# Attention and mixture of experts: another instruction order, V on two hardware rings, smaller weight pieces and later Q/K loads

## The chip, the cores and the metric

The kernel runs on one core of one Trainium2 chip. The metric is the device time of one execution, in microseconds (us); lower is better. A "fast" or "slow" run below is one run as against the fastest of the same kernel: a run over 1.5% above that is called slow, and ratios use fast runs only.

A core has a matrix engine (PE), a vector engine (DVE), an activation engine (ACT), a general engine (POOL) and a synchronization engine (SP). Sixteen DMA engines move data. In this kernel POOL, SP and ACT can start DMAs; each of the three has a queue of its own in the profile (q0 for POOL, made by software; q1 for SP and q10 for ACT, in hardware).

## The reference

Eight batches, eight heads, sequence 576, head size 64. Attention has a decay per position (a cumulative sum of logarithms of f); its output goes through one of eight experts, chosen per batch.

```python
log_f = np.log(np.clip(f, 0.0001, 1.0))
cum = np.cumsum(log_f, axis=-1)
scores = q @ k^T / 8 + cum[:, :, :, None] - cum[:, :, None, :]   # causal
attn = softmax(scores)
x = attn @ v                              # (8, 576, 512) over all heads
# mixture of experts, one expert per batch:
e_idx = np.argmax(x.mean(axis=1) @ w_gate, axis=1)
out[b] = gate[b] * (np.maximum(x[b] @ w1[e_idx[b]], 0) @ w2[e_idx[b]])
```

(Shortened; the exponentials of the decay are applied to V and to the row sums in the kernel.)

## The kernel before

The program writes its own instruction order. Each piece of work is an `Op` with an engine, a duration, what it waits for and a priority; `Order.run` simulates the engines and the transfers, takes at each moment the ready piece with the lowest priority number, and emits its instructions. A group is four heads of one batch, so there are 16 groups. The steps of a group are: load Q and K (POOL's queue), transpose them (DVE), scores (PE), exponentials (ACT), mask (POOL), V times the decay (POOL, "weighing"), PV (PE), normalization (ACT, DVE). After two groups comes the batch's gate (PE), then the load of the chosen expert's W1 and W2 (POOL's queue), then 128 matmuls of W1 and of W2 ("MoE").

```python
    def load_v(b, c):                       # five chunks per batch, all from SP
        t = VF[od.slot(("vf", b))]          # two buffers
        if c < 4:
            nc.sync.dma_start(t[:, c, :, :], v[b, :, P * c:P * c + P, :].rearrange("h p e -> p h e"))
        ...
    # [cut] Q/K loads: four buffers, on POOL's queue
    raws[g, j] = od.add(f"raw{g}{j}", "POOL", .6, ..., takes=(("raw", g),) ..., lands=1.55, ...)
    # [cut] W1 and W2 of a batch: 4 KB and 8 KB pieces, on POOL's queue too
    nc.gpsimd.dma_start(W1[w].rearrange("p (q t) n -> p q (t n)", t=2), src.rearrange("p q t n -> p q (t n)"))
    nc.gpsimd.dma_start(W2[w].rearrange("p m n -> p (m n)"), ...)
    # [cut]
    pm = 1000 + 20 * b                      # priority of the MoE: after everything else
    for g in range(5, NQ):
        raws[g, 1].behind = [ld2]           # Q/K of later groups only wait for batch 0's weights
```

## Time and profile before

| | before |
|---|---|
| median of three runs | 280.07 us (276.8 to 280.75); with a fourth, of 281.22 us, it is 280.41 |
| profiled run: span | 281.3 us |
| PE busy | 242.6 us, 86% |
| wait of POOL for V | 18.4 us |
| first gate, last gate, end | 36.0, about 225.7, 281.3 us |

The lines below are from the page of the kernel before: the span; the busy time of each engine; the busy tenths of PE, the granted clock of PE and the share of the DMA engines in 40 slices of the span; the two data queues (packets, megabytes, share of the time of 16 engines); the chain that ended last, by engine.

```profile
span 281.3 us, 7976 instructions
...
PE 242.6 (86%) x3351; PEld 156.6 (56%) x3351; DVE 110.7 (39%) x298; ACT 175.1 (62%) x263; POOL 115.2 (41%) x181
...
PE   8976898892299599939889999989999999999990
...
PEclk9995799997589999986979999999999999999997
DMA  6946929999999999989999954931593259603122
...
q0 software_dynamic: 8880, 26.22, 49.1%
q1 hardware_dynamic: 43744, 19.04, 27.8%
...
PE 62%; DMA 17%; ACT 7%; POOL 4%; issue 4%; DVE 2%; SPq 2%; POOLq 0%; ACTq 0%
```

PE is busy most of the time, but in the two slices from 63 to 77 us it is busy for only 2 tenths, and in the one from 120 to 127 us for 3; there the DMA row stands at 9. Another clue is the chain: 17% of the span is DMA.

The next lines are waits of the kernel before: engine, line and tile, then what it waited for, then us in total, how many times, and the longest.

```profile
POOL vb L374 <- DMA vf<-in_v_dram: 18.4, 4, 11.6
PE ps_w L390 <- POOL e L361: 15.2, 3, 7.6
...
PE ps_s L348 <- ACT e L354: 7.1, 8, 1.4
```

POOL waited four times for V, up to 11.6 us at once. The chain of work that ended last, in order of time (start, us, what), has the same loads in it:

```profile
43.77 26.98 DMA vf<-in_v_dram
...
104.17 19.87 DMA vf<-in_v_dram
```

By stretches of the span (start:end, length, busy time of PE, PEld, DVE, ACT and POOL with the number of instructions, granted clock, DMA share, GB/s):

```profile
44.00:71.00 27.00, 18.40 (x344) 12.89 (x337) 11.70 (x35) 16.90 (x23) 14.23 (x23) 0.92 1.13 203
71.00:80.00 9.00, 4.45 (x58) 2.65 (x58) 2.40 (x6) 2.41 (x4) 8.69 (x13) 0.50 1.03 192
98.00:160.00 62.00, 53.83 (x916) 35.59 (x919) 31.60 (x88) 44.35 (x60) 37.05 (x57) 0.92 1.07 227
160.00:226.00 66.00, 64.99 (x1004) 43.00 (x993) 33.05 (x92) 43.67 (x59) 21.70 (x34) 1.00 0.55 127
226.00:282.00 56.00, 48.54 (x342) 35.46 (x341) 2.25 (x8) 30.60 (x62) 1.27 (x2) 0.96 0.41 112
```

A DMA share over 1 means that packet times overlap. Up to 160 us the DMA engines are full and PE is not; from 71 to 80 us PE works for 4.45 of 9 us. After 160 us PE is full, and after 226 us only MoE is left: the last gate is followed by 55 us. The instances of the gate's matmuls (count; shortest, median and longest in ns; first and last start) give the ends of that count:

```profile
L470 PE MATMUL ps_w<-wg,pt x64: 172/256/277, 36.0 to 226.4; 128*128 128x8 f32 x64
```

From the timeline of PE, all eight gates start at 36.0, 62.8, 97.4, 119.7, 147.9, 169.6, 197.0 and 225.7 us. The start of the kernel is seen in two lines of PE's timeline (start, us, instruction):

```profile
12.53 0.52 PE L311 MATMUL ps_w<-identf,CUM 64*128 64x64 f32 x5
...
14.23 0.57 PE L348 MATMUL ps_s<-qt,kt 32*128 32x448 bf16 x8
```

The five transposes of the cumulative sum begin at 12.53 us, and the first scores at 14.23 us.

### The profile page before, as it was taken

The numbers are of one execution on the slowest core, as the hardware profiler recorded it, in microseconds if no ns is written. First come the engines' busy times: TensorE is split into PE (matmuls) and PEld (weight loads), VectorE is DVE, ScalarE is ACT, GpSimd is POOL, SyncE is SP. The second block draws the span as 40 slices with busy tenths as digits, with TensorE's granted clock in tenths as the row PEclk, the third lists the DMA queues.
The fourth block names the chain that finished last, engine by engine and source line by source line (L and its number), as shares of the span: only waits on it lengthen the run. The fifth ranks groups of instructions, "written<-read, shape, count | busy, mean of one in ns | idle before, by whom it ended". The sixth has DMA issues, their size and how long they took to land.

```text
span 281.3 us, 7976 instructions
## 1 busy us (share of the span) xinstructions
PE 242.6 (86%) x3351; PEld 156.6 (56%) x3351; DVE 110.7 (39%) x298; ACT 175.1 (62%) x263; POOL 115.2 (41%) x181
## 2 busy tenths in 40 slices
PE   8976898892299599939889999989999999999990
PEld 3433654661154367624356756765686597695940
DVE  4663535472043665604266554556453310000000
ACT  2189375972166797834868754886487677493930
POOL 4057159930888586435656534362231210000000
PEclk9995799997589999986979999999999999999997
DMA  6946929999999999989999954931593259603122
GB/s 120 227 72 127 228 37 200 209 207 197 199 202 203 217 289 218 215 200 212 230 256 209 214 149 102 231 82 58 128 229 68 87 112 221 213 2 130 41 94 81
DMA packets 52666, 45.84 MB, mean 163 GB/s; under 512 B 39376, under 2 KB 41424, under 8 KB 51728
## 3 DMA queue, kind: packets, MB, share of 16 engines
q0 software_dynamic: 8880, 26.22, 49.1%
q1 hardware_dynamic: 43744, 19.04, 27.8%
q8 instruction: 28, 0.46, 0.7%
q14 instruction: 14, 0.11, 0.1%
HBM read 62.03 MB, written 9.44 MB: 254 GB/s over the span
## 4 chain that ended last, share of the span: by engine, by line
PE 62%; DMA 17%; ACT 7%; POOL 4%; issue 4%; DVE 2%; SPq 2%; POOLq 0%; ACTq 0%
PE ps_w L525 19%; PE ps_w L511 17%; DMA vf<-in_v_dram 17%; PE ps_w L390 10%; PE ps_s L348 6%; ACT e L354 5%; PE ps_w L587 4%; PE ps_w L528 3%; PE ps_w L470 2%; ACT e L357 2%; SPq L250 2%; POOL e L361 1%; POOL vb L374 1%; PE ps_w L270 1%; PE ps_s L270 1%
## 5 line engine op out<-in xcount | busy, mean ns | idle before, releaser
L354 ACT ACTIVATE e<-ps_s 128x1792 bf16<-128x1792 f32 (+2 forms) x60 | 90.7, 1512 | 26.1 <-PE ps_s L348 24.3
L511 PE MATMUL ps_w<-xT,w1e 128*128 128x288 bf16 x512 | 72.6, 291 | 2.6 <-DMA w1e<-in_moe_w_dram 1.4
L511 PEld LDWEIGHTS <-w1e 128*128 128x128 bf16 x512 | 60.7, 142 | 13.6 <-issue 9.0
L361 POOL TENSOR_SCALAR_AFFINE_SELECT e<-e 128x512 bf16<-128x512 bf16 x64 | 40.7, 636 | 58.2 <-ACT e L354 56.5
L525 PE MATMUL ps_w<-w2e,h1T 128*128 128x512 bf16 x256 | 61.3, 390 | 0.0
L517 DVE TENSOR_SCALAR h1T<-ps_w,gate_b 128x288 bf16<-128x288 f32 x58 | 29.1, 512 | 58.0 <-PE ps_w L511 57.8
L374 POOL TENSOR_TENSOR vb<-vf,WF 128x512 bf16<-128x512 f32 x29 | 30.0, 1042 | 29.5 <-DMA vf<-in_v_dram 18.4
L348 PE MATMUL ps_s<-qt,kt 32*128 32x448 bf16 (+3 forms) x720 | 33.9, 288 | 8.5 <-ACT e L354 7.1
L525 PEld LDWEIGHTS <-h1T 128*128 128x128 bf16 x256 | 24.1, 101 | 30.3 <-issue 5.9
L519 ACT ACTIVATE h1T<-ps_w,gate_b 128x288 bf16<-128x288 f32 x70 | 34.0, 500 | 5.6 <-PE ps_w L511 5.3
L406 DVE SCALAR_TENSOR_TENSOR xT<-ps_w,lr 128x256 bf16<-128x256 f32 (+1 forms) x64 | 26.7, 452 | 26.6 <-ACT lr L400 22.9
L537 ACT COPY otile<-ps_w 128x512 f32<-128x512 f32 (+1 forms) x30 | 16.5, 550 | 30.9 <-PE ps_w L525 28.8
L390 PE MATMUL ps_w<-e,WB 128*32 128x192 bf16 (+4 forms) x512 | 19.3, 272 | 16.2 <-POOL e L361 15.2
L348 PEld LDWEIGHTS <-kt 32*128 32x128 bf16 x768 | 16.5, 95 | 27.4 <-issue 24.6
L390 PE MATMUL ps_w<-e,vb 128*32 128x320 bf16 (+4 forms) x1024 | 30.9, 264 | 0.3 <-DVE h1T L517 0.3
L339 DVE STREAM_TRANSPOSE kt<-rawk 128x576 f32<-128x576 f32 x16 | 20.0, 1252 | 26.1 <-PE ps_s L348 21.9
L395 ACT ACTIVATE lr<-ps_w 128x256 f32<-128x256 f32 (+1 forms) x32 | 13.3, 414 | 19.6 <-PE ps_w L390 19.6
L390 PEld LDWEIGHTS <-WB 128*32 128x32 bf16 x512 | 11.1, 102 | 25.4 <-issue 22.1
L390 PEld LDWEIGHTS <-vb 128*32 128x32 bf16 x1024 | 22.4, 102 | 3.1 <-issue 0.6
L339 DVE STREAM_TRANSPOSE qt<-rawq 128x576 f32<-128x576 f32 x16 | 19.9, 1246 | 1.4 <-DMA rawq<-in_q_dram 1.4
L587 PE MATMUL ps_w<-still 128*128 128x512 bf16 x69 | 16.3, 380 | 0.0
L400 ACT ACTIVATE lr<-lr 128x256 f32<-128x256 f32 (+1 forms) x32 | 14.2, 444 | 1.0
(58 smaller groups left out, 138.3 us busy)
## 6 DMA issues: line engine op xcount, KB each, us to landing
vf<-in_v_dram SPq DMA_DIRECT2D x32, 256.0 KB, 7.0
w2e<-in_moe_w_dram POOLq DMA_DIRECT2D x8, 1024.0 KB, 13.9
out_dram<-otile SPq DMA_DIRECT2D x32, 256.0 KB, 2.7
w1e<-in_moe_w_dram POOLq DMA_DIRECT2D x7, 1024.0 KB, 9.1
rawk<-in_k_dram POOLq DMA_DIRECT2D x16, 288.0 KB, 9.1
rawq<-in_q_dram POOLq DMA_DIRECT2D x16, 288.0 KB, 9.5
vf<-in_v_dram SPq DMA_DIRECT2D x8, 128.0 KB, 12.7
w1e<-in_moe_w_dram POOLq DMA_DIRECT2D x4, 256.0 KB, 7.3
```

Of the source, the lines that this page charges most:

```text
L339: nc.vector.transpose(dst, raw)
L348: nc.tensor.matmul(ps[h][:, col:col + i1 - i0], kt[32 * h:32 * h + 32, KLO[c]:KLO[c] + P, r], qt[32 * h:32 * h + 32, i0:i1, r], start=(r = ...
L354: nc.scalar.activation(e, PS_S[:, :, 0:WIDTH[s]], AF.Exp, scale=0.125)
L361: nc.gpsimd.affine_select(out=e[:, :, 0:128], in_=e[:, :, 0:128], pattern=[[0, 4], [1, 128]], channel_multiplier=-1, base=0, compare_op=AL ...
L374: eng.tensor_tensor(vb[:, c, :, :], vf[:, c, h, :], WF[:, b, c, h].unsqueeze(3).to_broadcast([P, 2, 4, D]), op=ALU.mult)
L390: nc.tensor.matmul(ps[32 * h:32 * h + 32, lo - i0:hi - i0], lhs, e[s][:, h, col:col + hi - lo], start=(n == 0), stop=(n == len(parts) - 1) ...
L406: nc.vector.scalar_tensor_tensor(XT[od.slot(("x", b))][:, mm, i0:i1], ps[:, 0:i1 - i0], LN_SCALE, LR[od.slot(("lr", (g, blk)))][:, 0:i1 - ...
L511: nc.tensor.matmul(ps[:, 0:288], lhs, xT[:, m, 288 * half:288 * half + 288], start=(m == 0), stop=(m == 3))
L517: nc.vector.tensor_scalar(dst, ps[:, 0:288], g[:, 0:1], 0.0, op0=ALU.mult, op1=ALU.max)
L519: nc.scalar.activation(dst, ps[:, 0:288], AF.Relu, scale=g[:, 0:1])
L525: nc.tensor.matmul(ps, h[:, j, P * sb:P * sb + P], w2[:, j, :], start=(j == 0), stop=(j == 7))
L587: od.filler = lambda i: nc.tensor.matmul(PS_W[i], still[:, 0:P], still[:, 0:512])
```

## The change

Its intent was to keep V from waiting behind other transfers, and to spread the MoE over the kernel. Cut to its core:

```diff
+PM0 = 10.0
+LAG = 2
 ... class Order: the fluid model of DMA time (transfer) is replaced
-    def transfer(self, queue, at, us):
+    def advance(self, now):        # queues SP, ACT, POOL take turns by descriptor;
+        ...                        # each queue has its own descriptor time ("grain")
+        busy["PE"] = 2.0           # and fillers cost .43 at first, .24 later
-    def load_v(b, c):
+    def load_v(op, b, c):
+        eng = nc.scalar if op.engine == "ACT" else nc.sync
-            loads_v[b, c] = od.add(f"v{b}{c}", "SP", 0.5, ...)
+            loads_v[b, c] = od.add(f"v{b}{c}", "ACT" if c % 2 else "SP", .4 if c % 2 else .5, ..., grain=.022)
-        for i in range(12):        # twelve fillers ahead of everything
-            nc.tensor.matmul(PS_S[:, i, :] if i < 4 else PS_W[i % 4], still[:, 0:P], still)
 ... W1 and W2 of batches 1 to 7: two DMAs each, packets of 2 KB
+            for q in range(2):
+                nc.gpsimd.dma_start(W1[w].rearrange("p (t q) n -> p q t n", t=2)[:, q], src[:, q])
+            for a in range(2):
+                nc.gpsimd.dma_start(W2[w].rearrange("p (b a c) n -> p a b (c n)", b=2, a=2)[:, a], src[:, a])
-        pm = 1000 + 20 * b
+        pm = PM0 + 6 * b           # units of W1: pm + .4 * j; of W2: pm + 3.4 + .5 * n
-                raws[g, 1].behind = [ld2]
+                raws[g, 1].behind = [ld2] if g < 6 else [wvs[g - LAG][0]]   # Q/K wait for V's weighing two groups earlier
 ... some durations of the model are re-measured
```

## The prediction

> **What bounds the kernel now.** The page: span 281.3 us, PE busy 242.6, of which 21 are filler matmuls. Real PE work is about 197 us, an estimate from durations in the chain of waits (0.49 us per four 288-column matmuls, 1.68 per 72 PV matmuls, 8.0 per output batch). The DMA queues took 49.1% + 27.8% + 1%, some 219 us. Neither alone explains 280. The table by stretches shows DMA share 1.03 to 1.13 from 44 to 160 us, with PE busy only 4.5 of 9 us at 71 to 80 (clock 0.50). The chain names V's load: 27.0 us at 43.8, 19.9 us at 104.2. From 160 us PE is 98% busy, and the span ends with 55 us of MoE alone, left over by its low priority.
>
> **Why V is slow.** The packet records show strict turns: at 66 to 75 us, some 80 packets per us of 2304 B (Q/K, 0.195 us each) alternate with 80 to 90 of V's 256 B (0.022 us); beside 4 KB weight packets V gets some 48. A batch of V is 288 packets per DMA engine: 6.3 us alone, 62 us against a Q/K stream (288 x 0.217). This agrees with the Trainium skill, "DMA: Bandwidth & Descriptors", section "Queues, rings and completion order": each DMA engine goes round robin between the queue rows that have work, by packet.
>
> **What the change does.**
> 1. Two V packets per software turn instead of one, and weight packets of 2 KB (about 0.17 us, half of the 4 KB packet's 0.353) instead of 4 and 8 KB (0.627). Estimate of V's rate: six times beside W2, 1.8 times beside Q/K.
> 2. Q/K loads wait for V's weighing two groups earlier, so no longer run ahead of V.
> 3. MoE is interleaved. After the last gate 20 + 48 + 64 + 48 MoE matmuls remain, about 26 us, against 55.
> 4. 20 fillers precede the first score matmul instead of 43; CUM was ready at 7.9 us, its transposes ran at 12.5 behind fillers. Saves 3 to 4 us.
> 5. Cost: 16 V issues on ACT. On SP the first two issues of a batch took 0.38 and 0.58 us, the next 2.9 and 10.8. With two per batch I expect about 0.5 each, 8 us of an engine 62% busy: off the path. Bytes are unchanged; W2's smaller packets add about 3 us of DMA work, POOL gets 14 more issues of about 0.6 us.
>
> **Sum.** Gate 0 at 33 us instead of 36. Per batch PE needs 24.6 us and DMA about 27 us of packet time (25 with overlap); I expect 26 per gate, so the last gate near 216 instead of 226, then 31 us plus waits for the last weights. **Predicted 250 us, 238 to 265.** Faster by over 2%: 0.93, within: 0.05, slower: 0.02.
>
> **What would show it.** (1) POOL's wait for V falls from 18.4 us to under 6; the chain holds little V; two 256 B packets per software packet. (2) DMA share less saturated before 160 us, higher after. (3) Last gate to end about 31 us. (4) First score matmul near 11 us. (5) V issues on ACT under 1 us. A new wait: MoE's first matmuls on w1e, 1 to 3 us in some batches, since they follow their gate by some 12 us of PE work, and w1e now takes 9.1 us to land.
>
> **What would make it wrong.** ACT issues that block for many us and hold up the exponentials; interleaved MoE stalling PE, which runs in order, on weights that land late, because every software byte shares one queue; DMA as the true bound (219 us plus start and tail), which would hold the time above 260.

Two readings of it need a note. The clock of the packet records begins 10.4 us before the span, so its "66 to 75 us" is 56 to 65 us of the span. And its "80 packets per us" are over all 16 engines.

## The result, and the profile after

The kernel after takes 264.94 us (median of four runs, 262.53 to 266.27). The ratio to the kernel before is 0.9469, with a 95% interval of 0.9364 to 0.9573. (Ratios here are the mean time of one kernel's fast runs over that of the other's of the same rounds, so they are not quite the ratios of the quoted medians.) The sign was right; the size was about half of the 30 us predicted: 264.94 lies at the top end of the range of 238 to 265.

The same lines of the page of the kernel after:

```profile
span 263.9 us, 7930 instructions
...
PE 235.2 (89%) x3325; PEld 152.6 (58%) x3325; DVE 110.9 (42%) x297; ACT 174.9 (66%) x261; POOL 128.2 (49%) x195
...
PE   7778998939999999499899976799999999999991
...
PEclk9975999988999999799999997999999999999998
DMA  6988979991999999954999998695997299049832
...
q0 software_dynamic: 13584, 26.22, 55.6%
q1 hardware_dynamic: 27104, 14.85, 22.5%
q10 hardware_dynamic: 16640, 4.20, 8.1%
...
PE 53%; DMA 21%; ACT 8%; DVE 6%; issue 6%; POOL 4%; POOLq 0%; ACTq 0%; SPq 0%; DVEq 0%
```

Three queues now carry data. POOL's queue has half again as many packets for the same megabytes. The holes of PE moved: instead of one at a quarter of the span, there are several small ones. The chain holds **more** DMA than before, 21% against 17%.

The waits after:

```profile
PE ps_s L370 <- ACT e L376: 15.1, 12, 4.1
...
ACT e L376 <- DMA vf<-in_v_dram: 4.7, 1, 4.7
ACT e L376 <- DMA out_dram<-otile: 4.5, 1, 4.5
```

There is no line for POOL's weighing and V any more: that wait is gone, as predicted. But ACT now waits for DMA, and PE for ACT, 15.1 us against 7.1 us. The chain names the places:

```profile
34.76 20.42 DMA vf<-in_v_dram
55.27 0.37 ACTq L274
55.70 1.67 ACT e L376
...
92.62 14.48 DMA out_dram<-otile
107.16 0.37 ACTq L274
107.58 1.46 ACT e L376
```

Read the two triples. At 34.76 us SP starts a piece of V that lands 20 us later; then at once ACT's sequencer (ACTq) spends 0.37 us on starting **another** piece of V, and only then comes the exponential. At 92.62 us SP starts a store of output; when it has landed, ACT again starts a piece of V, and the exponential follows. Neither exponential needs that DMA. The issue itself is short (0.37 us, as predicted); ACT stands still ahead of it. In ACT's timeline these two exponentials are marked as having waited 4.71 us and 4.53 us.

The instruction listing of the built program (no profile: engine, row, instruction, semaphores waited for) tells what they wait for:

```
SP  row 12  L274 DMACopy vf_84<-in_v_dram 128x8x64 [waits DMAHW5_49]                       issued 34.76, landed 55.18
ACT row 55  L274 DMACopy vf_85<-in_v_dram 128x8x64 [waits DMAHW5_49,DMAHW3_49,Pool_49]     issued 55.27
```

(The times at the right are read from the trace.) The program gives DMAs from SP and ACT together eight completion semaphores, DMAHW0 to DMAHW7, in turn. The ninth DMA uses the semaphore of the first again, and waits for it to have landed. The eighth DMA before ACT's at 55.27 is SP's at 34.76, a piece of V(2) that landed at 55.18 us; the eighth before the one at 107.16 is the store, which landed at 107.10. The other two waits of the first line were over by then, so the buffer of V is not what held ACT: DMAHW3's DMA had landed at 30.04 us, and an issue of SP that waits for the same count of Pool (the weighing that frees the buffer) went out at 46.21 us. This agrees with the Trainium skill, "DMA: Bandwidth & Descriptors", section "Anatomy of one DMA — SWDGE (gpsimd) path", which says that DMA engines do not wait on semaphores and that "any semaphore wait happens on the issuing sequencer before dispatch". The section is about DMAs from POOL; the trace shows the same for ACT, whose sequencer waits here, and all that stands behind it in ACT's order waits too (4.71 and 4.53 us).

The stretches between gates, and after the last:

```profile
30.00:62.00 32.00, 25.81 (x404) 15.99 (x403) 15.06 (x39) 21.50 (x27) 16.86 (x25) 0.95 0.97 172
62.00:87.00 25.00, 24.78 (x376) 16.86 (x375) 9.14 (x32) 18.05 (x29) 18.11 (x26) 1.00 0.92 187
87.00:117.00 30.00, 26.41 (x406) 16.10 (x406) 14.91 (x38) 19.68 (x26) 13.62 (x21) 0.94 1.09 224
...
144.00:178.00 34.00, 28.12 (x416) 17.57 (x416) 16.02 (x39) 22.49 (x29) 16.85 (x25) 0.95 0.98 189
178.00:231.00 53.00, 52.51 (x813) 36.44 (x811) 22.80 (x69) 39.61 (x60) 29.42 (x43) 1.00 0.73 152
231.00:264.00 33.00, 27.08 (x185) 18.24 (x184) 1.04 (x6) 15.78 (x33) 2.89 (x4) 0.97 0.59 138
```

```profile
L492 PE MATMUL ps_w<-wg,pt x64: 173/256/276, 30.3 to 231.3; 128*128 128x8 f32 x64
```

The gates start at 30.3, 61.5, 86.5, 117.5, 143.7, 178.3, 204.2 and 230.6 us. Four of the seven intervals are 25 to 26.5 us long, and three are 31.3, 31.0 and 34.6. The profile before: its run took 282.94 us, 1% over the median, so differences of one or two us are not to be read from it. The kernel gained 5.7 us up to the first gate and 22 us after the last one (33.3 against 55.6), and **lost** 10.6 us in between (200.3 against 189.7). MoE work has moved into the middle, so the middle has more to do; but it took 28.6 us per gate, where the prediction had 26. The stretch from the first gate to the last in one line:

```profile
30.30:230.60 200.30, 183.23 (x2806) 121.54 (x2805) 90.84 (x247) 140.24 (x196) 110.40 (x163) 0.97 0.91 180
```

So PE was busy for 183.2 us of it (5.9 of them fillers, matmuls whose result nobody uses) and idle for 17.1 us. The first scores are at 10.80 us:

```profile
9.73 0.49 PE L333 MATMUL ps_w<-identf,CUM 64*128 64x64 f32 x5 [1.48 <-DVE CUM L328]
...
10.80 0.57 PE L370 MATMUL ps_s<-qt,kt 32*128 32x448 bf16 x8 [0.20 <-DVE qt L361]
```

### The profile page after: what moved, and what is told of

The parts are those of the page before. It is cut to its first block, busy times and chain, and to the rows that moved or that the text cites. A ratio compares the mean times of both kernels' runs of the same rounds, so it can differ in the third digit from the quotient of the medians.

```text
span 263.9 us, 7930 instructions
## 1 busy us (share of the span) xinstructions
PE 235.2 (89%) x3325; PEld 152.6 (58%) x3325; DVE 110.9 (42%) x297; ACT 174.9 (66%) x261; POOL 128.2 (49%) x195
## 3 DMA queue, kind: packets, MB, share of 16 engines
q0 software_dynamic: 13584, 26.22, 55.6%
## 4 chain that ended last, share of the span: by engine, by line
PE 53%; DMA 21%; ACT 8%; DVE 6%; issue 6%; POOL 4%; POOLq 0%; ACTq 0%; SPq 0%; DVEq 0%
PE ps_w L535 18%; PE ps_w L550 14%; PE ps_w L412 9%; DMA vf<-in_v_dram 8%; DMA rawk<-in_k_dram 7%; PE ps_s L370 7%; DMA out_dram<-otile 5%; ACT e L376 5%; PE ps_w L553 2%; PE ps_w L492 2%; ACT e L379 2%; DVE kt L361 2%; DVE qt L361 1%; POOL vb L396 1%; PE ps_w L612 1%
## 5 line engine op out<-in xcount | busy, mean ns | idle before, releaser
L376 ACT ACTIVATE e<-ps_s 128x1792 bf16<-128x1792 f32 (+2 forms) x61 | 91.9, 1507 | 31.1 <-PE ps_s L370 18.0
L535 PE MATMUL ps_w<-xT,w1e 128*128 128x288 bf16 x512 | 74.4, 295 | 1.6 <-DMA w1e<-in_moe_w_dram 1.1
L535 PEld LDWEIGHTS <-w1e 128*128 128x128 bf16 x512 | 61.5, 143 | 11.0 <-issue 5.0
L550 PE MATMUL ps_w<-w2e,h1T 128*128 128x512 bf16 x256 | 60.1, 384 | 0.0
L370 PE MATMUL ps_s<-qt,kt 32*128 32x448 bf16 (+3 forms) x728 | 34.2, 291 | 15.6 <-ACT e L376 15.1
L543 ACT ACTIVATE h1T<-ps_w,gate_b 128x288 bf16<-128x288 f32 x72 | 35.4, 500 | 13.2 <-PE ps_w L535 12.6
L541 DVE TENSOR_SCALAR h1T<-ps_w,gate_b 128x288 bf16<-128x288 f32 x56 | 28.0, 511 | 32.7 <-PE ps_w L535 32.7
L550 PEld LDWEIGHTS <-h1T 128*128 128x128 bf16 x256 | 23.3, 98 | 29.6 <-issue 4.2
L412 PE MATMUL ps_w<-e,vb 128*32 128x320 bf16 (+4 forms) x1024 | 29.6, 257 | 2.4 <-DVE xT L428 1.2
L515 POOL DMA_DIRECT2D w1e<-in_moe_w_dram x14 | 10.4, 743 | 20.4 <-DVE gate_b L506 15.3
L412 PE MATMUL ps_w<-e,WB 128*32 128x192 bf16 (+4 forms) x512 | 17.8, 261 | 0.4 <-ACT lr L417 0.2
L412 PEld LDWEIGHTS <-WB 128*32 128x32 bf16 x512 | 10.6, 99 | 9.0 <-issue 7.1
## 6 DMA issues: line engine op xcount, KB each, us to landing
rawk<-in_k_dram POOLq DMA_DIRECT2D x16, 288.0 KB, 10.7
```

Source lines behind the costliest of these rows:

```text
L370: nc.tensor.matmul(ps[h][:, col:col + i1 - i0], kt[32 * h:32 * h + 32, KLO[c]:KLO[c] + P, r], qt[32 * h:32 * h + 32, i0:i1, r], start=(r = ...
L376: nc.scalar.activation(e, PS_S[:, :, 0:WIDTH[s]], AF.Exp, scale=0.125)
L412: nc.tensor.matmul(ps[32 * h:32 * h + 32, lo - i0:hi - i0], lhs, e[s][:, h, col:col + hi - lo], start=(n == 0), stop=(n == len(parts) - 1) ...
L535: nc.tensor.matmul(ps[:, 0:288], lhs, xT[:, m, 288 * half:288 * half + 288], start=(m == 0), stop=(m == 3))
L541: nc.vector.tensor_scalar(dst, ps[:, 0:288], g[:, 0:1], 0.0, op0=ALU.mult, op1=ALU.max)
L543: nc.scalar.activation(dst, ps[:, 0:288], AF.Relu, scale=g[:, 0:1])
```

## The experiments

The theory after the comparison: the second ring costs time through ACT's waits on the eight semaphores, and this is why the middle is slow. First rival: the DMA engines are simply full. Second rival: interleaved MoE stalls PE, which runs in order. Beside this stands the question which part carries the gain: the second ring, the small packets, the delay of Q/K, the start or the priorities. Where an expectation below names theories by letters, they are those of its own text. Ratios are to the kernel before on the same chip, with medians of 280.47 (e1 to e4), 277.81 (e5 to e8), 279.15 (e9 to e12), 279.70 (e13 to e15) and 280.37 us (e16). The calls ran on different chips, and these medians differ by up to 2.7 us, so a difference of that size between kernels of different calls is not to be read.

### e1: one chunk of V from ACT instead of two

```diff
-        eng = nc.scalar if op.engine == "ACT" else nc.sync
+        eng = nc.scalar if c == 1 else nc.sync
```

> The changed kernel with one edit: of V's five loads per batch only chunk 1 is issued from ACT; chunk 3 goes back to SP. Everything else, and the order, is as in the changed kernel (264.9 us). Theory A (ACT's second V issue waits for the landing of the eighth hardware DMA before it, and exponentials stand behind it: 4.7 us at 55 and 4.5 us at 107 in the changed kernel): both waits vanish from ACT, and the time falls by 4 to 9 us, to 256 to 261. Theory B (the DMA rings are full at that time anyway, so ACT's wait only shows it): 263 to 268. Theory C (the instruction order itself holds waits, such as 32 score matmuls in a row at 155 us): 263 to 266.

Measured: 273.8 us (271.0 to 275.34), ratio 0.9711 [0.9626, 0.9796]. It missed what each theory expected: half of the ACT issues do not make half of the loss, but **more** loss. Its waits of ACT for DMA:

```profile
ACT e L376 <- DMA vf<-in_v_dram: 7.9, 1, 7.9
...
ACT lr L417 <- DMA vf<-in_v_dram: 6.0, 1, 6.0
```

They grew from 9.2 to 13.9 us. In the trace ACT's two issues come at 56.77 and 110.54 us, right after the landing of the eighth DMA before each: a piece of V of SP's at 56.67 us (55.18 in the new kernel), and another at 110.44 us (107.10, the store, in the new kernel). So fewer DMAs from ACT do not mean less waiting; when the eighth DMA before lands decides. Why those landed later was not taken apart.

### e2: no chunk from ACT, same order

```diff
-        eng = nc.scalar if op.engine == "ACT" else nc.sync
+        eng = nc.sync
```

> The changed kernel with all V loads issued from SP, so one hardware ring as before; order, 2 KB weight packets, delayed Q/K loads and MoE order kept. Packets: one 256 B packet of V per software packet instead of two. If the second ring is what shortened V's waits (prediction's step 1): V lands later, POOL waits for V again by 5 us or more, time 270 to 280. Theory A: ACT's waits vanish (9 us), so part of the loss is made good: 260 to 268.

Measured: 258.39 us (257.02 to 260.89), ratio 0.9192 [0.9133, 0.9252]. The order is that of the new kernel; only the ring of 16 DMAs differs. ACT has no wait for DMA left, and the time falls by 6.5 us. That is under both ranges expected: the waits of ACT vanished as theory A had it, but POOL's wait for V did not come back, so there was no loss to set against. So the second ring, as the new kernel uses it, costs time. One long gap between gates stays (136.5 to 173.0 us), so that one isn't made by the rings.

### e3: the order's model knows the eight semaphores

The model lets a DMA from SP or ACT start only when the eighth before it has landed. Two rings and small packets stay.

```diff
+        self.hw = []
     ... in run(), for each ready op:
+                    if ready is not None and op.lands is not None and e != "POOL":
+                        for a in self.hw[-8:][:2 if <store of two DMAs> else 1] if len(self.hw) >= 8 else ():
+                            ready = None if a.end is None or ready is None else max(ready, a.end)
     ... when it is issued:
+                if e != "POOL":
+                    self.hw += [op] * (2 if <store of two DMAs> else 1)
```

> The changed kernel, with the eight completion semaphores of the hardware DMAs put into the order's own model: a hardware DMA may be issued there only when the eighth before it has landed. All loads, rings and packet sizes stay; only the order changes. Theory A: ACT waits for V issues fall from 11 us to under 3, time 253 to 261. Theory B and C: 262 to 270, as the order is only shuffled.

Measured: 254.29 us (251.49 to 256.6; two of the four runs fast, so there is no interval). It has no wait of ACT for DMA, and PE's wait for the exponentials is

```profile
PE ps_s L376 <- ACT e L382: 4.3, 9, 1.4
```

instead of 15.1 us. Theory A's range held. The gates run from 29.6 to 217.4 us, that is 26.8 us each, close to the 26 predicted:

```profile
29.60:217.30 187.70, 180.81 (x2800) 120.60 (x2800) 89.95 (x247) 139.74 (x195) 110.54 (x163) 0.99 0.97 195
```

Here PE is idle for only 6.9 us, and the DMA engines' share is 0.97: both are nearly full. The order was remade, so part of the 10.7 us can be a luckier order; e2, which keeps the order, puts some 6.5 us on them.

### e4: half of the weights (a wrong result)

```diff
-            for q in range(2):           # W1; the same for W2
+            for q in range(1 if b > 2 else 2):
```

> Wrong result on purpose: from batch 3 on only half of W1 and half of W2 is loaded, which takes some 27 us of packet time off the DMA engines; no instruction else changes. Theory B (DMA queues bound the middle of the kernel): the time falls by 8 us or more, to 250 to 257. Theory A and C: the first three batches, where ACT waited, are as before; less than 5 us, 260 to 265.

Measured: 264.27 us (262.63 to 270.2), ratio 0.9418 [0.9348, 0.9488]: 0.7 us less than the new kernel, with half of the bytes of the weights gone from the fourth batch on. The result is wrong, as meant. The range of theories A and C held. So from there on the volume of the DMAs is not the bound. The first batches, where the DMA share is high too, e4 leaves as they were; for them speaks that e3 and e11 move the same bytes in 254 and 253 us. So the first rival falls as the reason for 265 us. The gap between the fifth and sixth gates stays as well, so it comes neither from the rings nor from the volume, and most likely from the instruction order (there, PE has 32 score matmuls in a row, each eight waiting for an exponential to free PSUM, the memory that PE writes to). That this is the cause was not tried; it is only argued from the order.

### e5: the MoE at its old low priority

```diff
-        pm = PM0 + 6 * b        # .4 * j, 3.4 + .5 * n
+        pm = 1000 + 20 * b      # j, 9 + n
```

> The changed kernel with MoE's old priorities (after all attention) and everything else new. The built order still interleaves: after the last gate 32 + 48 + 64 + 48 MoE matmuls stand, not the 232 more of the kernel before. If the short end came from the priorities (prediction's step 3), the time rises to 275 to 285. If it comes from the queue model and the later Q/K loads, which hold attention back so that MoE fills in by itself: 256 to 270, with 33 to 36 us from the last gate to the end.

Measured: 259.19 us (256.63 to 259.93), ratio 0.9302 [0.9185, 0.9419]. The second expectation held. Without interleaving by priority the new kernel was 5.8 us **faster** by the medians (the two intervals overlap), and its tail was not long (last gate 221.8, end 256.6). But its ACT waited only 3.3 us for DMA, against 9.2 us. e12 and e16 take this up.

### e6: the Q/K loads are not delayed

```diff
-                raws[g, 1].behind = [ld2] if g < 6 else [wvs[g - LAG][0]]
+                raws[g, 1].behind = [ld2]
```

> The changed kernel with only the delay of the Q/K loads undone (they may go as soon as the first weights are issued and a buffer is free, as before). If that delay matters for V (step 2 of the prediction): V's wait returns on POOL (over 8 us) and the time rises to 272 to 285. If the two rings and small packets suffice: 260 to 268.

Measured: 281.84 us (280.97 to 283.64), ratio 1.0133 [1.0022, 1.0245]: the whole gain is gone, with two rings, small packets, the interleaved MoE and the new start all still in. The time is in the first range, but the sign named there is missing: POOL's weighing did not wait for V. ACT waited 7.7 us for V instead, so the 16.9 us mix two effects; e9 and e13 part them.

### e7: the old large weight packets

```diff
-            for q in range(2):
-                nc.gpsimd.dma_start(W1[w].rearrange("p (t q) n -> p q t n", t=2)[:, q], src[:, q])
+            nc.gpsimd.dma_start(W1[w].rearrange("p (q t) n -> p q (t n)", t=2), src.rearrange("p q t n -> p q (t n)"))
 ... the same for W2, and the indices of the matmuls as before
```

> The changed kernel, same order, with weights of batches 1 to 7 in packets of 4 and 8 KB again and one issue each instead of two. If small packets are what let V through (step 1): V's landings beside weights are later, time 270 to 280. If V mostly competes with Q/K packets, which are 2304 B in both, and half the weight issues (14 x 0.74 us) leave POOL: 261 to 267.

Measured: 263.76 us (263.58 to 267.12), ratio 0.9519 [0.9397, 0.9642]. That is within the spread of the new kernel: no gain of the 2 KB pieces is seen. One thing blurs this pair: ACT's wait for DMA was 2.9 us here, not 9.2, so large packets may have cost what the shorter wait gave. The pair e8 and e11, where ACT has no such wait in its exponentials, shows no gain either. (In e4 the wait was 4.1 us.) Over the five kernels with the same order the time from the first gate to the last goes with this wait, though not one for one: 192.6 us with none (e2), 197.5 with 2.9 (e7), 196.2 with 4.1 (e4), 200.3 with 9.2 (the new kernel) and 206.5 with 13.9 us (e1).

### e8: one ring, and the model knows the eight semaphores

e3, with all V ops on `"SP"`.

> Order made anew with all V loads on SP and with the eight semaphores in the model: no V issue on ACT at all. Against 254.3 us with two rings and the same model: if the second ring has a worth of its own once ACT no longer waits, this is slower by 3 us or more, 257 to 265. If the second ring was worth nothing, 251 to 256.

Measured: 253.76 us (253.68 to 256.59), ratio 0.9156 [0.9047, 0.9264]. Where ACT no longer waits, two rings (e3, 254.29) and one ring (253.76) are the same. The second expectation held: the second ring by itself carries no gain.

### e9: the kernel before, plus the delay of the Q/K loads

```diff
-                raws[g, 1].behind = [ld2]
+                raws[g, 1].behind = [ld2] if g < 6 else [wvs[g - 2][0]]
```

> The kernel before with one line of the change: from group 6 on, Q/K loads wait for V's weighing two groups earlier. Everything else is old: one ring for V, large weight packets, the old model, MoE by low priority. Theory A (the delay alone carries the gain, because Q/K no longer run ahead of V): POOL's wait for V falls from 18.4 us to under 6, the gates after the first come about 3 us sooner each, and the time is 258 to 266 us. Theory B (the delay pays only with an order that was made for it, the old model places V and Q/K wrongly and so builds stalls into the order): 270 to 285 us, with V's wait gone but PE waiting for Q/K or for the exponentials. The tail after the last gate should stay about as long as before in both (50 us or more), since the MoE is still left for last; if the tail is then about 33 us, the short tail of the new kernel comes from the delay.

Measured: 270.39 us (269.11 to 272.51), ratio 0.9667 [0.9604, 0.973]. This is the low end of the second range expected, and outside the first. The delay alone, with the old model, one ring, large packets and MoE last, gives 9 of the 15 us. V's wait fell, but not under 6:

```profile
POOL vb L377 <- DMA vf<-in_v_dram: 6.9, 1, 6.9
...
POOL vb L374 <- DMA vf<-in_v_dram: 5.2, 3, 2.8
```

That is 12.1 us against 18.4. The tail stayed long, as both theories had it: the last gate is at 215.7 us, the end at 270.8.

### e10: the new kernel with the old start

Twelve fillers at the front and the old cost of fillers in the model; the order of everything else is the same.

> The new kernel with the old start: twelve fillers ahead of everything and the old cost of a filler in the model. If the earlier first score matmul (10.8 against 14.3 us) is worth what the first gate shows, this is 3 to 5 us longer than the new kernel: 267 to 270 us, first gate near 34. If the start is absorbed by the load of V, the time stays within 1 us of 264.

Measured: 272.22 us (268.7 to 274.95), ratio 0.9685 [0.958, 0.9789]: 7.3 us more than the new kernel. That is more than either expectation. The first scores came at 14.77 us instead of 10.80, the first gate at 36.2 instead of 30.3. The start is worth more than the 3 to 4 us that the prediction gave it.

### e11: one ring, eight semaphores, large packets

e8 with e7's edit. Of the change there remain the delay, the new model, the start and the priorities.

> V all on one ring, the model knows the eight completion semaphores, weights in pieces of 4 and 8 KB as before: of the change there remain the delay of Q/K, the descriptor model, the start, and the MoE priorities. If rings and packet sizes are worth nothing, 252 to 256 us, as the same kernel with small packets (253.8). If small packets do protect V once there is one ring for it, 258 to 264 with a wait of POOL for V of over 4 us.

Measured: 252.79 us (252.11 to 255.26, six runs), ratio 0.9044 [0.8998, 0.909]. **This is the lowest median** (e8 and e3 lie within 1.5 us of it, so the three are hardly told apart), 12 us below the kernel after, and it has neither the second ring nor the small pieces. The first expectation held.

### e12: e8 with the MoE at its old priority

> V all on one ring, the model knows the eight completion semaphores, and the MoE has the old low priority. In the new kernel the old priority gained about 5 us. If that gain adds to the gain of one ring with eight semaphores (253.8), this is 247 to 251 us; if both gains are the same thing, namely that ACT's exponentials are held up less, this is 253 to 257 us.

Measured: 260.58 us (259.87 to 262.54), ratio 0.9327 [0.9282, 0.9372]. Both expectations missed: 6.8 us **more** than e8. Here the tail is long (last gate 213.9, end 261.0), and interleaving is a gain. With that the second rival loses its ground: in the new kernel PE waited 1.1 us for weights (w1e), and here keeping the MoE for last costs time.

### e13: e11 without the delay of the Q/K loads

> The kernel of e11 (one ring, eight semaphores in the model, large weight packets; 252.8 us) without the delay of the Q/K loads. In e6 the delay's removal cost 17 us, but there the activation engine also stood still for completions of slow V loads; in e9 the delay alone gave 9 us. Theory A (the delay matters because Q/K ahead of V starve it, whoever issues V): 260 to 270 us, and with the activation engine free of DMA waits. Theory B (the loss in e6 came through the activation engine's waits): 252 to 257 us, since no V is issued from that engine here.

Measured: 270.22 us (269.15 to 273.37), ratio 0.966 [0.9606, 0.9714]: 17.4 us more than e11, with no V on ACT. Theory A holds. The trace says how: V's third batch begins at about the same time in each kernel, and is complete at very different ones:

| kernel | first piece issued | last piece landed, us |
|---|---|---|
| before | 39.8 | 71.8 |
| e9 (before, with the delay) | 39.3 | 61.5 |
| e13 (e11 without the delay) | 36.1 | 85.7 |
| e11 | 34.2 | 57.3 |

Here the 17 us don't appear as a long wait of POOL for V (it waits 5.1 us for V altogether): the model foresaw the late V and put MoE in front. What is seen instead is an interval of 40 us between the second and third gates (60.4 to 100.4 us), where e11 has 22.7 us (57.8 to 80.5).

### e14: e11 with Q/K one group earlier

```diff
-LAG = 2
+LAG = 3
```

> The kernel of e11 with Q/K held back until V's weighing three groups earlier instead of two, so the loads may start one group sooner. The chain of e11 holds 14 per cent of waits on rawk. If Q/K now comes too late, 248 to 252 us and less of rawk in the chain; if the earlier load only takes turns from V, 253 to 260 us.

Measured: 260.99 us (259.44 to 266.34), ratio 0.934 [0.9301, 0.9378]: 8 us more than e11, just above the second range. The second range rested on Q/K taking V's turns. The trace does not show that: POOL does not wait for V, and V's third batch is complete at 59.2 us (57.3 in e11). The chain's share of Q/K loads (rawk) is 14%, as in e11; what grew is PE's wait for W1, from 1.1 to 4.3 us. The cause of the 8 us stays open.

### e15: the kernel before, plus the second ring

```diff
-            nc.sync.dma_start(t[:, c, :, :], ...)
+            (nc.scalar if c % 2 else nc.sync).dma_start(t[:, c, :, :], ...)
```

> The kernel before with one part of the change: chunks 1 and 3 of each V batch issued from the activation engine, same order, large packets. Theory A (V's rate was the bound and a second ring doubles its turns, as the prediction had it): POOL's wait for V falls from 18.4 us to under 10 and the time to 268 to 275 us. Theory B (what V gains is paid back as waits of the activation engine for the landing of an earlier hardware DMA, which here is slower than in the new kernel): over 275 us, with waits of the activation engine on DMA of 8 us or more in its exponentials.

Measured: 286.75 us (285.17 to 287.87), ratio 1.0271 [1.0222, 1.032]: slower. The waits:

```profile
PE ps_s L348 <- ACT e L354: 24.4, 12, 9.6
...
ACT e L354 <- DMA out_dram<-otile: 7.1, 1, 7.1
...
POOL vb L374 <- DMA vf<-in_v_dram: 1.7, 1, 1.7
```

V's wait is nearly gone (1.7 us against 18.4), just as the prediction's first step says, **and the kernel is slower**: PE waits 24.4 us for the exponentials instead of 7.1. ACT's timeline shows a V issue that took 6.56 us by itself, and the exponential behind it, whose idle time of 11.18 us is put down to "issue":

```profile
59.38 6.56 ACTq L250 DMA_DIRECT2D vf<-in_v_dram  x1
65.98 1.24 ACT L354 ACTIVATE e<-ps_s 128x1280 bf16<-128x1280 f32 x1 [11.18 <-issue]
```

The trace parts it: the eighth DMA before this issue, SP's piece of V of 39.71 us, landed at 59.28 us, and the issue began at 59.38. So some 4.6 us of the 11.18 are the wait for the semaphore, and 6.6 the issue itself. Here the danger that the prediction named, an issue that blocks, came true beside the wait in front of it. The range of theory B held.

### e16: e3 with the MoE at its old priority

> The kernel of e3 (two rings for V, small packets, the model knows the eight completion semaphores; 254.3 us) with the old low priority of the MoE. In the new kernel itself the old priority was 6 us better (e5, 259.2 against 264.9), with one ring and eight semaphores 7 us worse (e12, 260.6 against e8, 253.8). Theory A (interleaving is worth about 7 us, and e5 only gained because its order ran into shorter waits of the activation engine for DMA, 3.3 instead of 9.2 us): 259 to 263 us here, since these waits are gone in both. Theory B (the sign depends on the second ring, not on those waits): 246 to 253 us.

Measured: 256.94 us (256.34 to 259.74), ratio 0.9191 [0.9114, 0.9269]: 2.7 us more than e3 by the medians, and 5.3 by the means of the fast runs (257.5 against 252.2). It lies between the two ranges expected; its sign is that of the first. In both pairs where ACT doesn't wait for hardware DMAs in its exponentials, interleaving helps, by 3 to 7 us.

### What each part is worth

| part | pair of kernels | medians, us |
|---|---|---|
| delay of Q/K loads | before to e9 | 279.15 to 270.39 |
| the same, with ACT free of V | e13 to e11 | 270.22 to 252.79 |
| second ring | before to e15 | 279.70 to 286.75 |
| second ring | e2 to after | 258.39 to 264.94 |
| second ring, semaphores in the model | e8 to e3 | 253.76 to 254.29 |
| small weight packets | e7 to after | 263.76 to 264.94 |
| small weight packets | e11 to e8 | 252.79 to 253.76 |
| new start | e10 to after | 272.22 to 264.94 |
| MoE by priority, ACT waiting for DMA | e5 to after | 259.19 to 264.94 |
| MoE by priority, ACT not waiting | e12 to e8 | 260.58 to 253.76 |
| semaphores in the model | after to e3 | 264.94 to 254.29 |

In some pairs (delay, priority, model) the whole order is made anew, so a difference of a few us can belong to the new order rather than to the part. Pairs from different calls carry the difference of the chips too (up to 2.7 us by the kernel before). The values don't add up, because the parts act on each other. The pairs of e2, e7, e10 and e15 keep the order of all real work.

## Why the prediction was right or wrong

- **Bound by V behind Q/K: right.** Packets took strict turns. In 56 to 65 us of the span of before there were 79 packets of 2304 B (Q/K) and 87 of V's 256 B per us; after, in 82 to 90 us, 73 of Q/K and 82 of V on each of the two rings. This agrees with the skill's section "Queues, rings and completion order", which the prediction cites: each engine goes round robin between queue rows, by packet. POOL's wait for V fell from 18.4 us to nothing.
- **Step 1 as a source of time: wrong.** Twice the turns and 2 KB packets did what was computed, and were worth nothing once step 2 kept Q/K away from V (e3 and e8, e8 and e11). By itself step 1's second ring removed V's wait (18.4 to 1.7 us) and made the old kernel slower (e15). The wait that was removed was replaced by another, on the engine that now starts the DMA.
- **Step 2 was the main one, and had the least words.** The prediction put no number to it. Alone it gave 9 us (e9), and taking it away cost 17 us in two kernels (e6, e13). V's third batch landed 28 us earlier with it (85.7 to 57.3 us).
- **Step 3, the tail: size right, its value not what the sum took it for.** 33.3 us after the last gate, 31 predicted. But the work that left the tail went into the middle. Nor did the priority alone make the tail: with the old one it was 34.8 us in e5, 38.8 in e16 and 47.1 in e12 (end less last gate). Interleaving is worth 3 to 7 us where ACT doesn't wait; in the kernel as changed it cost 6 by the medians (e5), most likely because its order ran into longer waits of ACT (9.2 against 3.3 us).
- **Step 4, the start: right in kind, too small.** First scores at 10.80 us (about 11 predicted), first gate at 30.3 us instead of 33; worth 7 us (e10), not 3 to 4.
- **Step 5 failed.** It said of the V issues on ACT: "8 us of an engine 62% busy: off the path." They took 0.37 to 0.69 us each, 6.7 us in all, so the sign by which it was to be judged (issues under 1 us) came out true. The cost lay in front of them: 9.2 us of waiting for the landing of the eighth DMA before. "ACT issues that block for many us" was on the list of what could go wrong, but the check looked at the issue's duration and not at the idle time of the next instruction.
- **The term of the sum.** Predicted: 33 us to the first gate, 183 to the last (seven at 26), 31 after and 3 of waits. Measured: 30.3 + 200.3 + 33.3 = 263.9. The mis-sized term is the 26 per gate: it was 28.6. With ACT's waits out of the order (e3) it is 26.8, and the time is 254.3 us. So taking ACT's waits away, with the new order that this brings, removed 12.5 of the 17.3 us by which the middle was over (200.3 to 187.8, against 183). The rest is the need of PE itself, which the prediction put too low. It reckoned with 24.6 us of PE work per batch, so its 183 us left 10.8 us for waits. PE was busy for 26.2 us per gate in the new kernel and for 25.8 in e3 (0.8 and 0.9 of it fillers), and idle for 17.1 and 6.9 us. So of the 17.3 us over, 11.0 are PE's own busy time and 6.3 its waits; in e3 the waits were within what was allowed, and the 4.8 us that remain are busy time. (The granted clock between these gates was 0.97 and 0.99; what share of the busy time it holds, no run tells.) By luck the first gate, 2.7 us earlier than predicted, hid a part of the loss, so that the time still fell within the range.
- **DMA as the bound, the second danger named, did not come**: half of the late weights changed nothing (e4), and the same bytes went through in 254 us (e3), although packet time rose from 216 to 227 us (the shares of the data queues times the span).

What stays open: why the order of the new kernel has a gap of 34.6 us between the fifth and sixth gates that survives e2 and e4; and why V issues of SP and, in e15, one of ACT take 6 to 15 us themselves. Of SP's the runs show only that nothing was lost when all V issues went there (e2).

## What to carry to other kernels

Ask of a DMA that is moved to a compute engine not only how long its issue takes, but what it waits for before the issue, for example a completion semaphore that is used again in turn: everything behind it on that engine waits too, so look at the idle time of the next instruction. When one stream starves behind another that has run ahead, hold back the one that is early before giving the late one more turns; here one line did 9 of the 15 us by itself. And where a program orders itself by a model, a constraint that the model doesn't know (eight DMAs in flight) becomes a stall in the order; putting it in, with the new order that this brought, took 10.7 us off.

## What the Trainium skill lacked or had wrong

- "DMA: Bandwidth & Descriptors", section "Issuing engines are not separate DMA queues": it says that starting DMAs on several engines only saves the sequencer's time to initiate them. For the total that agrees (e3 with two rings 254.29 us, e8 with one 253.76). It does not say that a second row doubles the turns of one stream (82 + 82 V packets per us, against 87 with one ring), though that follows from the arbitration in the section named last below. And it lacks that this can cost time: 286.75 against 279.70 us in e15, since the compute engine waits before the issue and in it.
- The same page, section "Why a DMA increments its semaphore by 16 and not by 1": "One semaphore per in-flight slot, not one per stream." The built program follows this with eight semaphores for SP and ACT together. The page lacks what follows for the order: the ninth DMA waits for the landing of the first, on the engine that issues it (4.71 and 4.53 us in the new kernel, 13.9 us in e1).
- No page used has a number for an issue that blocks by itself: up to 14.9 us on SP and 6.56 us on ACT here, beside 0.37 to 0.69 us for the V issues of ACT in the new kernel.
- The same page, section "Queues, rings and completion order", was right, and round robin by packet was sufficient to compute V's rate (79 packets of Q/K and 87 of V per us). How many pieces make up a turn these counts do not tell, as long as both queues have the same number.
